# A fourth weight quarter taken for two token pairs at once: 512 columns in place of twice 256, and three zero products less

## Chip, core and metric

The kernel runs on one core of one Trainium2 chip. The time is that of one execution on the device in microseconds. TensorE (PE in the profile) makes all products, PEld is its loading of weights; VectorE is DVE, ScalarE is ACT, GpSimd is POOL, SyncE is SP.

## What is computed

Attention within chunks of 64 tokens, for 8 batches, 8 heads, 576 tokens and a head width of 64, and behind it a feed-forward part on the 4608 tokens of width 512:

```python
scores = scale * np.matmul(q_c, k_c.transpose(0, 1, 2, 4, 3))
attn = np.exp(scores - np.max(scores, axis=-1, keepdims=True))
attn = attn / (np.sum(attn, axis=-1, keepdims=True) + 1e-09)
x = np.matmul(attn, v_c)           # then (B, S, H * D) rows: 4608 x 512
a = x @ w1                         # 512 x 1024
b = x @ w2                         # 512 x 1024
out = (a * b @ w3) @ w_out         # 1024 x 1024, 1024 x 512
```

Inputs and output are float32; the products are made in bfloat16 with float32 sums.

## The kernel before

The tokens are cut into 18 pairs of 256 (p = 0 to 17; a pair is two units of 128, u = 0 and 1), and two pairs make a group of 512 tokens. The work is written out by hand as one list of steps, ORDER, which is walked from left to right; every engine and every DMA queue gets its instructions in that order. A step is a letter with numbers:

- `q`, `k`, `v`: loads of a pair, issued by POOL, with a cast to bfloat16. `i0` to `i3`: one quarter of the columns (256) of w1 and of w2 each. `h0`, `h1`: halves of w3, and `o`: w_out, each as four DMAs that fill 32 partitions each. POOL issues all of them in the order of the list.
- `R`, `K`: pair 0's q and k by another way (SP, ACT and a cast). `T`: VectorE transposes q (T p.0) or k (T p.1). `G`, `H`: moves on the SP queue, from pair 6 (MOVED) on.
- `S`: scores on TensorE; `E`: exponential on ScalarE; `P`: times v, on TensorE; `N`: VectorE divides; `X`: VectorE transposes to x with its width on the partitions, one unit at a time.
- `A p.j` and `B p.j`: x times w1 into the first PSUM bank of a tile, x times w2 into the second. `C`: ScalarE copies the first bank to SBUF; `M`: VectorE multiplies it with the second into the tile `ab` of the group (bfloat16).
- `V`, `W`, `Z`: w3 times w_out is made once (w3 transposed by VectorE in V, products on TensorE in W, copied in Z), so that `O` makes the output from `ab` with one product; `Y` copies it and `Q` stores it.
- `D which.p.j.n.cols`: n products of zeros on TensorE, into the PSUM tile that the next real step overwrites. Nothing reads them.

The width of w1 and w2 is 8 blocks of 128 (f = 0 to 7), their depth 4 blocks. For the pairs 0 to 3, a step A p.j or B p.j takes two blocks, f = 2j and 2j + 1 (the quarter j of the weights), for the 256 tokens of one pair: 8 products of 128x256, each with a weight load of its own. From pair 4 on, a step takes one block f = j for the 512 tokens of a group: 4 products of 128x512. Both fill one bank with 512 float32 per partition. PSUM is four tiles of two banks, taken in turn, so a step that begins such a tile waits for what read the tile four before it.

The helper `mm` (L97) makes every product, and `load` (L100) every load by POOL. The list around the change: the zero products D1.0.0.6.512 stand ahead of A0.0; A0.3, B0.3 (pair 0, fourth quarter) stand around S2, behind A0.2, A1.0, B0.2, A1.1, B1.0 and B1.1; A1.2, A1.3, B1.2 and B1.3 follow P2.

Of the kernel before, what the change touches and what calls it, by code (L numbers as in the profile page):

```python
# [7 lines left out]

ORDER = """
R0.0 R1.0 R0.1 R1.1 v0 D0.0.1.9.512 K0.0 K1.0 T0.0.0 K0.1 T0.1.0 K1.1 S0.0 T0.0.1 E0.0 T0.1.1 q1 k1  # L10
S0.1 i0 E0.1 P0.0 P0.1 T1.0 D0.1.0.6.512 v1 N0.0 T1.1 N0.1 X0.0 X0.1 i1 i2 S1 E1 D1.0.0.6.512 A0.0
C0.0 P1 B0.0 q2 N1.0 X1.0 N1.1 A0.1 C0.1 k2 B0.1 M0.0 A0.2 X1.1 A1.0 i3 C0.2 B0.2 M0.1 A1.1 v2 q3
B1.0 B1.1 M0.2 C1.0 C1.1 T2.0 k3 A0.3 C0.3 T2.1 S2 E2 B0.3 M1.0 M1.1 P2 M0.3 N2.0 N2.1 A1.2 C1.2
X2.0 A1.3 X2.1 C1.3 T3.0 B1.2 q4 T3.1 v3 k4 B1.3 A2.0 M1.2 C2.0 B2.0 S3 E3 T4.0 A2.1 M1.3 B2.1 M2.0
P3 A2.2 h0 N3.0 N3.1 B2.2 X3.0 A2.3 C2.1 C2.2 X3.1 o M2.1 C2.3 B2.3 A3.0 C3.0 M2.2 B3.0 V0 h1 A3.1
A3.2 q5 k5 C3.1 M2.3 B3.1 B3.2 v4 V1 C3.2 q6 T4.1 V2 V3 M3.0 W0 S4 k6 q7 M3.1 Z0 M3.2 V4 V5 W1 T5.0
Z1 W2 V6 V7 T5.1 W3 T6.0 E4 k7 q8 v5 Z2 A3.3 k8 q9 k9 Z3 S5 T6.1 T7.0 q10 T7.1 E5 v6 v7 C3.3 P4 B3.3
N4.0 X4.0 M3.3 O0 G3.0 N4.1 k10 Y0 G3.1 T8.0 O1 X4.1 P5 T8.1 Y1 O2 Q0 N5.0 N5.1 X5.0 v8 X5.1 A4.0 S6
E6 T9.0 T9.1 S7 B4.0 T10.0 Y2 q11 O3 C4.0 M4.0 Q1 E7 P6 v9 N6.0 A4.1 N6.1 C4.1 Y3 B4.1 A4.2 X6.0
M4.1 G4.0 A4.3 X6.1 C4.2 P7 N7.0 C4.3 B4.2 G4.1 k11 B4.3 N7.1 X7.0 A4.4 M4.2 B4.4 Q2 M4.3 C4.4 T10.1  # L20
M4.4 A4.5 C4.5 S8 B4.5 A4.6 C4.6 A4.7 E8 B4.6 Q3 C4.7 X7.1 B4.7 M4.5 q12 P8 H3.0 M4.6 S9 H3.1 M4.7
O4 E9 T11.0 Y4 P9 N8.0 O5 k12 N8.1 A6.0 B6.0 Y5 T11.1 G5.0 T12.0 A6.1 X8.0 N9.0 B6.1 C6.0 C6.1 T12.1
A6.2 q13 X8.1 B6.2 N9.1 X9.0 M6.0 k13 C6.2 v10 T13.0 v11 X9.1 M6.1 A6.3 M6.2 q14 G5.1 C6.3 A6.4 q15
B6.3 C6.4 B6.4 A6.5 S10 C6.5 B6.5 T13.1 M6.3 M6.4 A6.6 H4.0 E10 P10 H4.1 M6.5 S11 N10.0 B6.6 k14
N10.1 v12 A6.7 C6.6 E11 G6.0 P11 M6.6 N11.0 B6.7 X10.0 N11.1 A8.0 A8.1 B8.0 G6.1 C6.7 C8.0 B8.1 A8.2
B8.2 C8.1 M6.7 T14.0 q16 A8.3 M8.0 C8.2 M8.1 X10.1 M8.2 X11.0 Q4 q17 T14.1 H5.0 B8.3 C8.3 S12 S13
X11.1 A8.4 E12 C8.4 B8.4 k15 H5.1 M8.3 E13 v13 k16 A8.5 B8.5 P12 M8.4 k17 v14 T15.0 N12.0 N12.1 O6
A8.6 v15 C8.5 C8.6 T15.1 Y6 T16.0 B8.6 A8.7 M8.5 C8.7 P13 Q5 M8.6 B8.7 X12.0 A10.0 C10.0 B10.0 N13.0
N13.1 M8.7 G7.0 A10.1 T16.1 C10.1 A10.2 X12.1 X13.0 M10.0 C10.2 G7.1 B10.1 B10.2 A10.3 B10.3 C10.3
M10.1 T17.0 A10.4 C10.4 M10.2 M10.3 A10.5 T17.1 B10.4 M10.4 X13.1 v16 H6.0 S14 C10.5 S15 G8.0 B10.5  # L30
M10.5 O7 G8.1 E14 E15 P14 A10.6 H6.1 N14.0 C10.6 B10.6 A10.7 N14.1 Q6 Y7 M10.6 P15 N15.0 N15.1 C10.7
X14.0 S16 B10.7 M10.7 O8 E16 Q7 A12.0 B12.0 C12.0 M12.0 Y8 A12.1 C12.1 P16 S17 N16.0 X14.1 B12.1 E17
A12.2 M12.1 B12.2 A12.3 C12.2 A12.4 B12.3 X15.0 B12.4 v17 C12.3 M12.2 A12.5 N16.1 B12.5 M12.3 H7.0
X15.1 A12.6 X16.0 A12.7 C12.4 M12.4 C12.5 M12.5 C12.6 P17 N17.0 Q8 B12.6 B12.7 M12.6 H7.1 A14.0
A14.1 C12.7 B14.0 N17.1 C14.0 M12.7 O9 B14.1 C14.1 Y9 A14.2 X16.1 M14.0 M14.1 C14.2 A14.3 B14.2 Q9
O10 B14.3 X17.0 H8.0 Y10 Q10 A14.4 C14.3 A14.5 X17.1 C14.4 B14.4 M14.2 B14.5 H8.1 M14.3 A14.6 O11
Y11 B14.6 M14.4 O12 C14.5 C14.6 Y12 A14.7 M14.5 A16.0 C14.7 C16.0 Q11 M14.6 B14.7 A16.1 C16.1 A16.2
B16.0 B16.1 M14.7 M16.0 C16.2 M16.1 Q12 A16.3 O13 B16.2 B16.3 A16.4 C16.3 M16.2 Y13 M16.3 C16.4
A16.5 A16.6 B16.4 A16.7 C16.5 B16.5 M16.4 O14 Y14 C16.6 B16.6 C16.7 M16.5 B16.7 M16.6 Q13 M16.7 O15
Y15 O16 Q14 Q15 Y16 Q16 O17  # L40
"""


# [5 lines left out]
def first_path(  # L49
# [22 lines left out]
    FO = DF // P  # L72
# [19 lines left out]
    def inorder(ins):  # L92
        tc.keep_in_program_order(ins)
        return ins

    def mm(*a, **kw):
        return inorder(nc.tensor.matmul(*a, **kw))  # L97
# [4 lines left out]
    def psum(name):  # L102
        return ps.tile([P, 2, 512], f32, tag="p", name=name)
# [89 lines left out]
    qkT_t, qkm_t, s_t, e_t, pv_t, xn_t, xm_t, xt_t = {}, {}, {}, {}, {}, {}, {}, {}  # L193
# [101 lines left out]
    def new_xt(g):  # L295

        if g not in xt_t:
            xt_t[g] = asb.tile([P, KO * GT], bf, tag="xt", bufs=4, name="xt")
        return xt_t[g]
# [24 lines left out]
    ab_t, ps_t, a_t, o_t = {}, {}, {}, {}  # L324

    def do_D(which, p, j, n, cols):

        d, key = ((s_t, (p, (None, 0)[j])), (ps_t, (p, j)), (pv_t, (p, 0)))[which]
        if key not in d:
            d[key] = psum("z_ps")  # L330
        for _ in range(n):
            mm(d[key][:, 0, 0:cols], lhsT=zero[:, 0:P], rhs=zero[:, 0:cols], start=True, stop=True)

    def do_AB(p, j, f, which):

        if p >= MOVED:
            rhs = new_xt(p // 2)[:].rearrange("p (s o t) -> p o s t", s=2, o=KO)
        else:
            rhs = new_xt(p // 2)[:].rearrange("p (o t) -> p o t", o=KO)
            if p < 4:  # L340
                rhs = rhs[:, :, p % 2 * PT:(p % 2 + 1) * PT]
        fs = (f,) if p >= 4 else (2 * j, 2 * j + 1)
        n = GT // len(fs)
        for i, f in enumerate(fs):
            for ki in range(KO):
                ins = mm(ps_t[p, j][:, which, i * n:(i + 1) * n],
                         lhsT=(w1, w2)[which][:, ki, f * P:(f + 1) * P], rhs=rhs[:, ki],
                         start=(ki == 0), stop=(ki == KO - 1))
                if which == 1:
                    if (p, j) in first:  # L350
                        two_banks(ins, first[p, j])
                    else:
                        second.setdefault((p, j), []).append(ins)
# [3 lines left out]
    def two_banks(a, b):  # L357

        tc.declare_no_dep(a.ins, b.ins, reason="w1's product is read in one bank, w2's is made in the next")

    def do_A(p, j):
        ps_t[p, j] = ps_t.pop((p, j)) if (p, j) in ps_t else psum("ab_ps")
        do_AB(p, j, j, 0)

    def do_B(p, j):
        do_AB(p, j, j, 1)
# [7 lines left out]
    def do_M(p, j):  # L374
        g = p // 2
        if g not in ab_t:
            ab_t[g] = msb.tile([P, FO, GT], bf, tag="ab", bufs=3, name="ab")
        if p < 4:
            o = ab_t[g][:, 2 * j:2 * j + 2, p % 2 * PT:(p % 2 + 1) * PT]
            view = lambda t: t.rearrange("p (j t) -> p j t", j=2)  # L380
        elif p < MOVED:
            o = ab_t[g][:, j]
            view = lambda t: t
        else:
            o = ab_t[g][:, j].rearrange("p (c s y) -> p s c y", s=2, y=BL)
            view = lambda t: t.rearrange("p (s c y) -> p s c y", s=2, y=BL)
        inorder(nc.vector.tensor_mul(o, view(a_t.pop((p, j))[:]), view(ps_t.pop((p, j))[:, 1, :])))  # L387
# [66 lines left out]
    def load_half3(i):  # L454
# [9 lines left out]

    do = {"q": load_q, "k": load_k, "v": load_v, "i": load_w12, "o": load_wo, "h": load_half3, "T": do_T, "S": do_S, "R": do_R, "K": do_K, "E": do_E, "w": do_w, "x": do_x, "G": do_G, "H": do_H,
          "P": do_P, "N": do_N, "X": do_X, "A": do_A, "B": do_B, "C": do_C, "M": do_M, "D": do_D, "V": do_V,
          "W": do_W, "Z": do_Z, "O": do_O, "Y": do_Y, "Q": do_Q}
    for step in ORDER.split():
# [88 lines left out]
def kernel(tc, *args):  # L557
    second_path(tc, first_path(tc, *args), *args)
# [30 lines left out]
```

## Time and profile before

| | before |
|---|---|
| median of 3 runs | 241.46 us (240.96 to 241.86) |
| the profiled execution | 241.66 us, its span 240.1 us |
| mean granted TensorE clock | 0.985 |
| busy: PE, PEld, DVE | 230.6, 120.2, 152.3 us |
| busy: ACT, POOL | 84.7, 83.4 us |
| products ab_ps of 128x256, of 128x512 | 240, 448 |
| DMA moved | 39.21 MB |

The profile is one execution. A row of a timeline has the start, the length, the engine, the line, the operation with its output and inputs, their shape, the number of instructions in a row and, in brackets, the idle time ahead and what ended it. A name z_ps is a PSUM tile that zero products have opened. A product's end is modelled, so the length of a group holds a tail behind the last one. "A <- B: t, n, m" in the waits reads: A waited for B, t us in total, n times, m the longest. In the table of stretches stand, behind the stretch, its length, the busy time and count of PE, PEld, DVE, ACT and POOL, the granted clock, the DMA share and GB/s. "DMA to landing" is the time from the issue of a load to its last byte.

### The profile page before, as it was taken

The page shows a single profiled execution, that of the slowest core. Times are in us where ns is not written, and L with a number is a line of the kernel's source. Part 1 is how long each engine was busy: PE and PEld are TensorE (multiplying, and loading weights), DVE is VectorE, ACT ScalarE, POOL GpSimd, SP SyncE. Part 2 cuts the span into 40 slices and gives each one's busy share as a digit, 9 for nine tenths or more (in the row PEclk, how much of TensorE's full clock was granted, in tenths as well). Part 3 has the DMA queues.
Part 4 walks back from the last instruction along what each step waited for, and adds up shares of the span by engine and source line. Part 5 has one row for each costly group of instructions (what it writes and reads, how often), then busy time and mean ns, then how long its engine had stood idle before and what let it go on. Part 6 is the DMA issues. An engine that isn't in the chain of part 4 may idle for free.

```text
span 240.1 us, 6225 instructions
## 1 busy us (share of the span) xinstructions
PE 230.6 (96%) x2621; PEld 120.2 (50%) x2621; DVE 152.3 (63%) x237; ACT 84.7 (35%) x119; POOL 83.4 (35%) x112
## 2 busy tenths in 40 slices
PE   5699999999999999999999999999999999999994
PEld 1367788744645444444544444454444444444442
DVE  2766799959979596998599798474773222223200
ACT  4322334214412544333526143355332213521322
POOL 7846865647852424775543520000000000000000
PEclk9679999999999999999999999999999999999999
DMA  6999999999999999999999999860410442202224
GB/s 177 179 185 188 178 175 199 202 188 174 174 220 242 236 224 253 201 204 196 212 222 222 214 252 152 190 210 3 131 48 3 131 131 87 90 0 89 85 90 175
DMA packets 94397, 39.21 MB, mean 163 GB/s; under 512 B 75296, under 2 KB 86816, under 8 KB 94368
## 3 DMA queue, kind: packets, MB, share of 16 engines
q0 software_dynamic: 82592, 18.88, 84.8%
q1 hardware_dynamic: 10720, 19.41, 27.6%
q10 hardware_dynamic: 1056, 0.52, 0.8%
q8 instruction: 20, 0.33, 0.5%
q14 instruction: 9, 0.07, 0.1%
HBM read 38.80 MB, written 9.44 MB: 201 GB/s over the span
## 4 chain that ended last, share of the span: by engine, by line
PE 55%; DMA 31%; POOL 5%; DVE 3%; issue 2%; SPq 2%; ACT 1%; DVEq 0%; POOLq 0%
PE ab_ps L97 34%; PE o_ps L97 17%; DMA qk<-in_k_dram 17%; DMA w<-in_moe_w_dram 7%; DMA qk<-in_q_dram 4%; DMA qkm<-qkT 3%; POOL vbuf L100 2%; SPq L199 2%; PE s_ps L97 2%; POOL qk L100 2%; PE pv L97 2%; DVE ab L387 1%; POOL w L100 1%; DVE xn L272 1%; DVE qkT L207 1%
## 5 line engine op out<-in xcount | busy, mean ns | idle before, releaser
L97 PE MATMUL ab_ps<-xt,w 128*128 128x512 bf16 (+1 forms) x688 | 128.7, 342 | 0.5 <-DMA w<-in_moe_w_dram 0.5
L97 PEld LDWEIGHTS <-w 128*128 128x128 bf16 x704 | 67.0, 98 | 54.9 <-DMA w<-in_moe_w_dram 1.3
L387 DVE TENSOR_TENSOR ab<-a_sb,ab_ps 128x512 bf16<-128x512 f32 x71 | 47.0, 673 | 53.8 <-PE ab_ps L97 30.2
L370 ACT COPY a_sb<-ab_ps 128x512 f32<-128x512 f32 x71 | 41.4, 587 | 73.8 <-PE ab_ps L97 73.0
L97 PE MATMUL o_ps<-w3o,ab 128*128 128x512 bf16 (+2 forms) x296 | 64.8, 373 | 0.5 <-issue 0.3
L207 DVE STREAM_TRANSPOSE qkT<-qk 128x1024 bf16<-128x1024 bf16 (+1 forms) x38 | 45.8, 1232 | 5.5 <-ACT qk L150 3.7
L97 PEld LDWEIGHTS <-ab 128*128 128x128 bf16 x296 | 28.4, 98 | 33.6 <-issue 1.0
L100 POOL DMA_DIRECT2D vbuf<-in_v_dram x40 | 33.8, 847 | 23.2 <-DMA qk<-in_k_dram 5.9
L417 ACT COPY o_sb<-o_ps 128x1024 f32<-128x1024 f32 x17 | 17.2, 1014 | 43.8 <-PE o_ps L97 43.4
L272 DVE TENSOR_TENSOR xn<-pv,rcs 128x512 bf16<-128x512 f32 x36 | 24.9, 691 | 1.2
L100 POOL DMA_DIRECT2D qk<-in_q_dram x23 | 18.0, 783 | 15.8 <-DVE ab L387 4.8
L100 POOL DMA_DIRECT2D qk<-in_k_dram x23 | 17.9, 781 | 11.1 <-DMA qk<-in_k_dram 4.1
L240 ACT ACTIVATE e<-s_ps 128x1024 bf16<-128x1024 f32 (+1 forms) x17 | 16.9, 1000 | 11.4 <-PE s_ps L97 11.2
L313 DVE STREAM_TRANSPOSE xm<-xn 128x512 bf16<-128x512 bf16 x24 | 16.3, 689 | 0.1
L97 PE MATMUL w_ps<-wo,w3T 128*128 128x512 bf16 x64 | 14.1, 379 | 0.1
L269 DVE RECIPROCAL rcs<-pv 128x8 f32<-128x8 f32 x36 | 6.9, 192 | 11.4 <-PE pv L97 11.4
L291 POOL CROSS_LANE_REDUCE all_good<-good 128x1 f32<-128x1 f32 x1 | 0.4, 354 | 39.6 <-DVE both L289 39.6
L100 POOL DMA_DIRECT2D w<-in_moe_w_dram x16 | 11.1, 696 | 5.7 <-DMA w<-in_moe_w_dram 3.9
L97 PEld LDWEIGHTS <-e 64*32 64x32 bf16 (+1 forms) x768 | 7.8, 101 | 6.9 <-issue 4.4
L428 DVE STREAM_TRANSPOSE w3T<-w 128x1024 bf16<-128x1024 bf16 x8 | 9.5, 1210 | 2.4 <-DMA w<-in_moe_w_dram 2.4
L97 PE MATMUL pv<-vbuf,e 64*32 64x65 bf16 (+1 forms) x768 | 10.1, 198 | 0.3 <-ACT e L240 0.2
L97 PEld LDWEIGHTS <-w3T 128*128 128x128 bf16 x64 | 6.1, 98 | 7.5 <-issue 0.4
(28 smaller groups left out, 56.3 us busy)
## 6 DMA issues: line engine op xcount, KB each, us to landing
out_dram<-o_sb SPq DMA_DIRECT2D x17, 512.0 KB, 3.0
qkm<-qkT SPq DMA_DIRECT2D x48, 128.0 KB, 7.0
vbuf<-in_v_dram POOLq DMA_DIRECT2D x32, 128.0 KB, 11.1
w<-in_moe_w_dram POOLq DMA_DIRECT2D x16, 256.0 KB, 9.1
xt<-xm SPq DMA_DIRECT2D x48, 64.0 KB, 5.8
qk<-in_q_dram POOLq DMA_DIRECT2D x11, 256.0 KB, 9.0
qk<-in_k_dram POOLq DMA_DIRECT2D x11, 256.0 KB, 12.1
wo<-in_moe_w_out_dram POOLq DMA_DIRECT2D x4, 256.0 KB, 9.4
```

What stands on the lines that cost most here:

```text
L97: return inorder(nc.tensor.matmul(*a, **kw))
L100: return inorder(nc.gpsimd.dma_start(dst, src))
L199: inorder(nc.sync.dma_start(dst, src))
L207: inorder(nc.vector.transpose(qkT_t[g][:, :, p % 2, s, heads(h)].rearrange("p e h (y t) -> p h t e y", t=2), qk_t[p][:, s, heads(h)].rearr ...
L240: inorder(nc.scalar.activation(e_t[p][:, :, heads(hh)], s_t[p, hh][:].rearrange("p u (h q) -> p u h q", q=CH)[:, :, heads(hh)], Exp, scale ...
L269: inorder(nc.vector.reciprocal(rc, pv[:, :, :, D:W]))
L272: inorder(nc.vector.tensor_mul(xn_t[p][:, u], pv[:, :, :, 0:D], rc.to_broadcast([P, 2, 4, D])))
L313: inorder(nc.vector.transpose(xm_t[g][:, u, :, m].rearrange("p o (c y) -> p c o y", y=BL), xn_t[p][:].rearrange("p u r m d -> p (u r) m d" ...
L370: first[p, j] = inorder(nc.scalar.copy(a_t[p, j][:], ps_t[p, j][:, 0, :]))
L387: inorder(nc.vector.tensor_mul(o, view(a_t.pop((p, j))[:]), view(ps_t.pop((p, j))[:, 1, :])))
L417: inorder(nc.scalar.copy(o_sb[:], ps_t.pop(p)[:]))
L428: inorder(nc.vector.transpose(w3T_t[f][:].rearrange("p k (f y) -> p f k y", y=BL), w3[:, NB * f:NB * (f + 1), :].rearrange("p f (k x) -> p ...
```

## The change

For the pairs 0 to 3 a step A, B, C or M with j of 4 or more now stands for the whole group: it takes one block, f = j - 4, in 512 columns. So A0.10 and A0.11 are the blocks 6 and 7 (the fourth quarter) for the pairs 0 and 1 together. In the list, A1.2 with its B, C and M stands where A0.3 stood, A0.10 where A1.2 stood, and A0.11 where A1.3 stood; A0.3 and A1.3 are gone. The pairs 2 and 3 keep their steps. D1.0.0 makes three zero products instead of six. The new form of the key in `do_D` gives the same keys for the steps in the list.

```diff
-S0.1 i0 E0.1 P0.0 P0.1 T1.0 D0.1.0.6.512 v1 N0.0 T1.1 N0.1 X0.0 X0.1 i1 i2 S1 E1 D1.0.0.6.512 A0.0
+S0.1 i0 E0.1 P0.0 P0.1 T1.0 D0.1.0.6.512 v1 N0.0 T1.1 N0.1 X0.0 X0.1 i1 i2 S1 E1 D1.0.0.3.512 A0.0
 C0.0 P1 B0.0 q2 N1.0 X1.0 N1.1 A0.1 C0.1 k2 B0.1 M0.0 A0.2 X1.1 A1.0 i3 C0.2 B0.2 M0.1 A1.1 v2 q3
-B1.0 B1.1 M0.2 C1.0 C1.1 T2.0 k3 A0.3 C0.3 T2.1 S2 E2 B0.3 M1.0 M1.1 P2 M0.3 N2.0 N2.1 A1.2 C1.2
-X2.0 A1.3 X2.1 C1.3 T3.0 B1.2 q4 T3.1 v3 k4 B1.3 A2.0 M1.2 C2.0 B2.0 S3 E3 T4.0 A2.1 M1.3 B2.1 M2.0
-P3 A2.2 h0 N3.0 N3.1 B2.2 X3.0 A2.3 C2.1 C2.2 X3.1 o M2.1 C2.3 B2.3 A3.0 C3.0 M2.2 B3.0 V0 h1 A3.1
+B1.0 B1.1 M0.2 C1.0 C1.1 T2.0 k3 A1.2 C1.2 T2.1 S2 E2 B1.2 M1.0 M1.1 P2 M1.2 N2.0 N2.1 A0.10 C0.10
+X2.0 A0.11 X2.1 C0.11 T3.0 B0.10 q4 T3.1 v3 k4 B0.11 A2.0 M0.10 C2.0 B2.0 S3 E3 T4.0 A2.1 M0.11 B2.1
+M2.0 P3 A2.2 h0 N3.0 N3.1 B2.2 X3.0 A2.3 C2.1 C2.2 X3.1 o M2.1 C2.3 B2.3 A3.0 C3.0 M2.2 B3.0 V0 h1
...
     def do_D(which, p, j, n, cols):
-        d, key = ((s_t, (p, (None, 0)[j])), (ps_t, (p, j)), (pv_t, (p, 0)))[which]
+        d, key = ((s_t, (p, 0 if j == 1 else None)), (ps_t, (p, j)), (pv_t, (p, 0)))[which]
...
+    def single(p, j):
+        return p < 4 and j < FO // 2
+
     def do_AB(p, j, f, which):
+        if j >= FO // 2 and p < 4:
+            f = j - FO // 2
...
-            if p < 4:
+            if single(p, j):
                 rhs = rhs[:, :, p % 2 * PT:(p % 2 + 1) * PT]
-        fs = (f,) if p >= 4 else (2 * j, 2 * j + 1)
+        fs = (2 * j, 2 * j + 1) if single(p, j) else (f,)
...
     def do_M(p, j):
-        if p < 4:
+        if single(p, j):
             o = ab_t[g][:, 2 * j:2 * j + 2, p % 2 * PT:(p % 2 + 1) * PT]
             view = lambda t: t.rearrange("p (j t) -> p j t", j=2)
         elif p < MOVED:
-            o = ab_t[g][:, j]
+            o = ab_t[g][:, j - FO // 2 if p < 4 else j]
```

More of the change, by code (lines that the diff above doesn't have):

```diff
@@ L15 @@
-P3 A2.2 h0 N3.0 N3.1 B2.2 X3.0 A2.3 C2.1 C2.2 X3.1 o M2.1 C2.3 B2.3 A3.0 C3.0 M2.2 B3.0 V0 h1 A3.1
[L16 to L40, printed above, removed]
+B1.0 B1.1 M0.2 C1.0 C1.1 T2.0 k3 A1.2 C1.2 T2.1 S2 E2 B1.2 M1.0 M1.1 P2 M1.2 N2.0 N2.1 A0.10 C0.10
@@ new lines @@
+X2.0 A0.11 X2.1 C0.11 T3.0 B0.10 q4 T3.1 v3 k4 B0.11 A2.0 M0.10 C2.0 B2.0 S3 E3 T4.0 A2.1 M0.11 B2.1
+M2.0 P3 A2.2 h0 N3.0 N3.1 B2.2 X3.0 A2.3 C2.1 C2.2 X3.1 o M2.1 C2.3 B2.3 A3.0 C3.0 M2.2 B3.0 V0 h1
+A3.1 A3.2 q5 k5 C3.1 M2.3 B3.1 B3.2 v4 V1 C3.2 q6 T4.1 V2 V3 M3.0 W0 S4 k6 q7 M3.1 Z0 M3.2 V4 V5 W1
+T5.0 Z1 W2 V6 V7 T5.1 W3 T6.0 E4 k7 q8 v5 Z2 A3.3 k8 q9 k9 Z3 S5 T6.1 T7.0 q10 T7.1 E5 v6 v7 C3.3 P4
+B3.3 N4.0 X4.0 M3.3 O0 G3.0 N4.1 k10 Y0 G3.1 T8.0 O1 X4.1 P5 T8.1 Y1 O2 Q0 N5.0 N5.1 X5.0 v8 X5.1
@@ new lines @@
+A4.0 S6 E6 T9.0 T9.1 S7 B4.0 T10.0 Y2 q11 O3 C4.0 M4.0 Q1 E7 P6 v9 N6.0 A4.1 N6.1 C4.1 Y3 B4.1 A4.2
+X6.0 M4.1 G4.0 A4.3 X6.1 C4.2 P7 N7.0 C4.3 B4.2 G4.1 k11 B4.3 N7.1 X7.0 A4.4 M4.2 B4.4 Q2 M4.3 C4.4
+T10.1 M4.4 A4.5 C4.5 S8 B4.5 A4.6 C4.6 A4.7 E8 B4.6 Q3 C4.7 X7.1 B4.7 M4.5 q12 P8 H3.0 M4.6 S9 H3.1
+M4.7 O4 E9 T11.0 Y4 P9 N8.0 O5 k12 N8.1 A6.0 B6.0 Y5 T11.1 G5.0 T12.0 A6.1 X8.0 N9.0 B6.1 C6.0 C6.1
+T12.1 A6.2 q13 X8.1 B6.2 N9.1 X9.0 M6.0 k13 C6.2 v10 T13.0 v11 X9.1 M6.1 A6.3 M6.2 q14 G5.1 C6.3
@@ new lines @@
+A6.4 q15 B6.3 C6.4 B6.4 A6.5 S10 C6.5 B6.5 T13.1 M6.3 M6.4 A6.6 H4.0 E10 P10 H4.1 M6.5 S11 N10.0
+B6.6 k14 N10.1 v12 A6.7 C6.6 E11 G6.0 P11 M6.6 N11.0 B6.7 X10.0 N11.1 A8.0 A8.1 B8.0 G6.1 C6.7 C8.0
+B8.1 A8.2 B8.2 C8.1 M6.7 T14.0 q16 A8.3 M8.0 C8.2 M8.1 X10.1 M8.2 X11.0 Q4 q17 T14.1 H5.0 B8.3 C8.3
+S12 S13 X11.1 A8.4 E12 C8.4 B8.4 k15 H5.1 M8.3 E13 v13 k16 A8.5 B8.5 P12 M8.4 k17 v14 T15.0 N12.0
+N12.1 O6 A8.6 v15 C8.5 C8.6 T15.1 Y6 T16.0 B8.6 A8.7 M8.5 C8.7 P13 Q5 M8.6 B8.7 X12.0 A10.0 C10.0
+B10.0 N13.0 N13.1 M8.7 G7.0 A10.1 T16.1 C10.1 A10.2 X12.1 X13.0 M10.0 C10.2 G7.1 B10.1 B10.2 A10.3
@@ new lines @@
+B10.3 C10.3 M10.1 T17.0 A10.4 C10.4 M10.2 M10.3 A10.5 T17.1 B10.4 M10.4 X13.1 v16 H6.0 S14 C10.5 S15
+G8.0 B10.5 M10.5 O7 G8.1 E14 E15 P14 A10.6 H6.1 N14.0 C10.6 B10.6 A10.7 N14.1 Q6 Y7 M10.6 P15 N15.0
+N15.1 C10.7 X14.0 S16 B10.7 M10.7 O8 E16 Q7 A12.0 B12.0 C12.0 M12.0 Y8 A12.1 C12.1 P16 S17 N16.0
+X14.1 B12.1 E17 A12.2 M12.1 B12.2 A12.3 C12.2 A12.4 B12.3 X15.0 B12.4 v17 C12.3 M12.2 A12.5 N16.1
+B12.5 M12.3 H7.0 X15.1 A12.6 X16.0 A12.7 C12.4 M12.4 C12.5 M12.5 C12.6 P17 N17.0 Q8 B12.6 B12.7
+M12.6 H7.1 A14.0 A14.1 C12.7 B14.0 N17.1 C14.0 M12.7 O9 B14.1 C14.1 Y9 A14.2 X16.1 M14.0 M14.1 C14.2
@@ L41 @@
+A14.3 B14.2 Q9 O10 B14.3 X17.0 H8.0 Y10 Q10 A14.4 C14.3 A14.5 X17.1 C14.4 B14.4 M14.2 B14.5 H8.1
+M14.3 A14.6 O11 Y11 B14.6 M14.4 O12 C14.5 C14.6 Y12 A14.7 M14.5 A16.0 C14.7 C16.0 Q11 M14.6 B14.7
+A16.1 C16.1 A16.2 B16.0 B16.1 M14.7 M16.0 C16.2 M16.1 Q12 A16.3 O13 B16.2 B16.3 A16.4 C16.3 M16.2
+Y13 M16.3 C16.4 A16.5 A16.6 B16.4 A16.7 C16.5 B16.5 M16.4 O14 Y14 C16.6 B16.6 C16.7 M16.5 B16.7
+M16.6 Q13 M16.7 O15 Y15 O16 Q14 Q15 Y16 Q16 O17
 """
```

## The prediction, made before the changed kernel had run

> **What bounds the kernel now.** I read the page's busy line and slices first, then TensorE's waits, TensorE's order of time around the change, and last the loads that its waits name.
>
> ```profile
> span 240.1 us, 6225 instructions
> PE 230.6 (96%) x2621; PEld 120.2 (50%) x2621; DVE 152.3 (63%) x237; ACT 84.7 (35%) x119; POOL 83.4 (35%) x112
> PE   5699999999999999999999999999999999999994
> PEclk9679999999999999999999999999999999999999
> ```
>
> TensorE is busy for 96% of the span, and the slices (6 us each) show its idle time at the two ends. The granted clock (PEclk, in tenths) is low in the second and third slice alone. So the kernel is bound by TensorE's work, plus whatever short waits stand in its row. The change lies at 14 us and between 26 and 36 us; which waits of TensorE stand near there and behind?
>
> ```profile
> PE ab_ps L97 <- DMA w<-in_moe_w_dram: 0.5, 2, 0.3
> PE s_ps L97 <- DMA qkm<-qkT: 0.4, 1, 0.4
> ```
>
> One line is for the weights w1 and w2 (two waits), one for the moved q and k of a later group. TensorE in order of time (start, length, what; idle before and its releaser in brackets):
>
> ```profile
> 14.02 1.70 PE L97 MATMUL z_ps<-zero 128*128 128x512 bf16 x6
> 15.56 1.04 PE L97 MATMUL z_ps<-xt,w 128*128 128x256 bf16 x8
> 18.04 2.10 PE L97 MATMUL ab_ps<-xt,w 128*128 128x256 bf16 x16
> 20.43 5.42 PE L97 MATMUL ab_ps<-xt,w 128*128 128x256 bf16 x48 [0.29 <-DMA w<-in_moe_w_dram]
> 26.04 1.05 PE L97 MATMUL ab_ps<-xt,w 128*128 128x256 bf16 x8 [0.20 <-DMA w<-in_moe_w_dram]
> 27.02 0.71 PE L97 MATMUL s_ps<-qkT 32*64 32x64 bf16 x64
> 28.87 0.70 PE L97 MATMUL pv<-vbuf,e 64*32 64x65 bf16 x64 [0.16 <-ACT e L240]
> 29.50 5.41 PE L97 MATMUL ab_ps<-xt,w 128*128 128x256 bf16 x48
> 38.22 8.91 PE L97 MATMUL ab_ps<-xt,w 128*128 128x256 bf16 x80
> 47.25 3.61 PE L97 MATMUL w_ps<-wo,w3T 128*128 128x512 bf16 x16
> 139.07 10.54 PE L97 MATMUL ab_ps<-xt,w 128*128 128x512 bf16 x48
> ```
>
> The length of a group holds the tail of its last product, so I take the pace from differences: (8.91 - 5.41) / 32 = 0.109 us (0.1094) for 256 columns, and (10.54 - 3.61) / 32 = 0.217 us (0.2166) for 512. The group at 18.04 is A0.1 and B0.1; the one at 20.43 is A0.2, A1.0, B0.2, A1.1, B1.0, B1.1; the one at 26.04 is A0.3; 27.02 is S2, 28.87 is P2, and 47.25 is W0, the first product of w3 and w_out. A0.2 and A0.3 each begin when a quarter of w1 lands; nothing on TensorE sets their time.
>
> **Three zero products fewer.** They stand ahead of A0.0. Which clock do they run at, and what is A0.0's next condition?
>
> ```profile
> 7.60:7.80 0.20, 0.00 (x0) 0.00 (x0) 0.20 (x2) 0.20 (x1) 0.20 (x1) 0.77 1.99 174
> 13.00:14.00 1.00, 1.00 (x65) 0.93 (x64) 0.97 (x3) 0.00 (x0) 0.36 (x1) 0.50 2.19 153
> 14.20:14.60 0.40, 0.40 (x2) 0.15 (x1) 0.40 (x2) 0.40 (x1) 0.00 (x0) 0.58 2.44 155
> 14.60:14.80 0.20, 0.20 (x3) 0.10 (x1) 0.20 (x1) 0.20 (x1) 0.00 (x0) 1.00 2.25 164
> 13.68 1.29 DVE L305 STREAM_TRANSPOSE xt<-xn 128x512 bf16<-128x512 bf16 x2
> ```
>
> The third number from the end of a stretch is the granted clock: it falls near 7.7, is 0.50 until about 14.53 (0.58 over 14.20 to 14.60 is 0.33 us at 0.50 and 0.07 at 1.00), then 1.00. At half speed a product takes 2 x 0.217 = 0.43 us, so of the six the first ends at 14.45, the second, partly at full clock, at about 14.71, and four at 0.217 follow to 15.56, as the trace has it. With three, the last ends at 14.92. A0.0 then waits for X0.1, whose transposes end at 13.68 + 1.29 = 14.97; with some 0.07 us for the signal it starts near 15.05, 0.51 us earlier. Of 0.65 us of products, 0.14 becomes idle.
>
> Next come P1 (after E1), B0.0, A0.1, B0.1 and A0.2. Their weights land when they did:
>
> ```profile
> 19.08 0.77 PEld L97 LDWEIGHTS <-w 128*128 128x128 bf16 x8 [0.29 <-DMA w<-in_moe_w_dram]
> 20.42 5.14 PEld L97 LDWEIGHTS <-w 128*128 128x128 bf16 x48 [0.57 <-DMA w<-in_moe_w_dram]
> 17.98 0.76 POOL L100 DMA_DIRECT2D w<-in_moe_w_dram  x1 [0.57 <-DMA w<-in_moe_w_dram]
> ```
>
> B0.1's weights arrive at 19.08 and A0.2's at 20.42, both awaited already: A0.1 was through at 18.04 + 8 x 0.1094 = 18.92, 0.16 before, and B0.1 at 19.96, 0.47 before A0.2 began. The loads are issued by POOL, which waits for earlier loads to land (the last row, the fourth quarter's first issue), not for TensorE. So the 0.51 us is all waited away at A0.2: this part is worth 0 at 20.43. If A0.2 were not held, it would be worth up to 0.51.
>
> By the Trainium skill ("TensorE: Matmul & The Clock Gate", Part 1: The HAM clock gate) the clock is released after about 3.4 us of sustained activity, counted in a free-running window, which speaks against removing work that keeps TensorE warm. Here the three removed products lie after the rise at 14.53, so by the trace they did not earn it; what the rule would make of another phase is the clock rival below.
>
> **The fourth quarter in 512 columns.** A0.3, B0.3, A1.3 and B1.3 (32 products of 256 columns, 32 weight loads) become A0.10, B0.10, A0.11 and B0.11 (16 of 512, 16 loads): 32 x 0.1094 = 3.50 against 16 x 0.2166 = 3.47 us, a gain of 0.03, because the loads already ran beside the products. C and M stay four, each over 512 columns as before; PSUM tiles, DMAs and the other engines' steps keep number and order. M0.10 writes one row of 512 instead of two of 256, which I price at nothing; either form is bounded by M's 0.65 to 0.69 us.
>
> **The new order.** A1.2 stands where A0.3 stood. It needs the third quarter, which B0.2 used at about 22, and X1. So the wait for the fourth quarter at 26.04 goes: the 48 products from 20.43 are through at 20.43 + 48 x 0.1094 = 25.68, and A1.2 starts then, 0.36 us earlier. Then S2 could start at 26.56 instead of 26.92, if its transposes are through:
>
> ```profile
> 23.93 2.48 DVE L207 STREAM_TRANSPOSE qkT<-qk 128x1024 bf16<-128x1024 bf16 x2
> ```
>
> They end at 26.41, so 0.15 us is left. E2, B1.2 and P2 follow S2 as before, P2's short wait for E2 with them; A0.10 comes after P2, at about 29.1, three microseconds after its weights (26.0). So from 26 to 47 us TensorE is 0.36 + 0.03 = 0.39 us early; the ends are 0, if S2 or the next transposes hold it back, and 0.39, which I take, as no row holds it.
>
> **What is late next.** W0 needs all four quarters of w_out, since each fills 32 of the 128 partitions, and V0 needs the whole first half of w3. Their last loads:
>
> ```profile
> 35.87 1.71 POOL L100 DMA_DIRECT2D wo<-in_moe_w_out_dram  x3 [0.37 <-DMA vbuf<-in_v_dram]
> L100 POOL DMA_DIRECT2D wo<-in_moe_w_out_dram x1: 576/576/576, 37.0 to 37.0; - x1
> DMA to landing us min/median/max: 10.1/10.1/10.1
> ...
> L100 POOL DMA_DIRECT2D w<-in_moe_w_dram x1: 642/642/642, 33.7 to 33.7; - x1
> DMA to landing us min/median/max: 8.3/8.3/8.3
> ```
>
> The first three rows are w_out's, the last two w3's. w_out is complete at 37.0 + 10.1 = 47.1, and W0 starts at 47.25, though the 80 products ahead of it were through at 38.22 + 80 x 0.1094 = 46.97. So W0 stood waiting for 0.28 us for a load that POOL issued when an earlier load landed. If TensorE arrives 0.39 earlier, it waits 0.67 and W0 starts at 47.25 again. The whole gain of this change on TensorE ends there; nothing on TensorE goes round this wait.
>
> What can still pass is what runs beside it. V0's data land at 33.7 + 8.3 = 42.0, and from V0 the chain of waits leads on:
>
> ```profile
> 42.18 1.21 DVE w3T L428
> ...
> 44.38 0.87 POOL qk L100
> 45.25 10.11 DMA qk<-in_k_dram
> ...
> 106.38 7.69 DMA qkm<-qkT
> ...
> 114.20 0.67 PE s_ps L97 x31
> ```
>
> VectorE could reach V0 0.39 earlier, but the load lets it begin only about 0.1 earlier; the loads of pair 5 follow 0.1 earlier, and TensorE's wait of 0.4 us for qkm, which ends at 114.20, where this chain meets it, could shrink by that 0.1. The ends are 0 and 0.4; I take 0.1, since the load's landing leaves no more.
>
> **The sum.** Zero products 0 (up to -0.51), order and width 0 at W0 (up to -0.39), the later wait -0.1: 241.66 - 0.1 = 241.56 us for the profiled execution (span 240.1, 1.56 us around it). That execution stood 0.2 above the median of the runs, 241.46; on the median the forecast is 241.36, told as **241.4 us**. 0.5% is 1.2 us, about what a measurement of this kernel can tell from no change (its three runs lie within 240.96 to 241.86).
>
> **Rivals.**
>
> *The gains come through.* If in the runs that are timed the loads land earlier than in this trace, the waits at 20.43 and 47.25 hold nothing, and 0.51 + 0.39 = 0.90 us come through, with the 0.1 at most 1.0: 240.5 us (241.46 - 1.0), or 241.1 if only the second wait gives way. For it: W0's wait is only 0.28 us long. Against it: both waits are in the trace, each on a load whose issue waits for other loads. As 240.5 is 0.4% below before, only a little more, in the transfers, makes it faster by over 0.5%.
>
> *Transfers collide later (slower).* If POOL's loads from 44.38 on go out earlier, the move of q and k at 106.38 shares its way with more of them. It took 7.69 us; POOL's loads took between 8.3 us (w3's fourth above) and 10.1 us (w_out's last) here, by how much was under way. A move that takes 10.1 - 8.3 = 1.8 us longer reaches TensorE at 115.9 instead of 114.06, and nothing later makes that good, as TensorE is busy from there on: 241.46 + 1.8 = 243.3 us. It decides as soon as the move lands later than 114.06, since S waits for it already. Against it: the order of all issues is the same, and the shift is only 0.1 us.
>
> *The clock rises later (slower).* If the three products were needed, the clock would stay at 0.50 for some time after 14.53. From 14.92 on, half of that time is lost. The waits for loads give 0.51 + 0.16 + 0.47 = 1.14 us of it back by A0.2, and those at A1.2's place and at W0 another 0.36 + 0.28. Another 3.4 us (half of the 6.8 from fall to rise), to 17.9, loses 1.5 us and costs nothing; 6.8 us, to 21.3, loses 3.2 and costs 3.2 - 1.14 - 0.64 = 1.4 us: 242.9 us. It decides from a rise after 14.92 + 2 x 1.78 = 18.5 us. Against it: with three products TensorE's row has no gap beyond the 0.14 us ahead of A0.0. By the same section of the Trainium skill the clock falls again only after an idle window; the trace agrees, in that PEclk stays at 9 or more over all the short waits from the fourth slice on.
>
> *The change doesn't do what it says.* X0.1 is late in the changed kernel, and the three products turn into idle time ahead of A0.0: 241.5 us, as before.
>
> **How the numbers follow.** Forecast 0.53, all within 0.5%. Gains come through 0.27: 0.17 faster by over 0.5%, 0.10 within. Transfers collide 0.10, slower. Clock 0.05: 0.03 slower, 0.02 within. Not what it says 0.05, within. Together: faster 0.17, same 0.53 + 0.10 + 0.02 + 0.05 = 0.70, slower 0.13. The range reaches down to the 240.5 of the first rival and, for the scatter of the runs, 0.1 further, 240.4; upward to 242.2, the highest run shown (241.86) and part of the way to the slower rivals. Below it lies some 0.08, above it 0.12.
>
> **What would show it.** In the changed profile: A0.0 near 15.05; A0.2 again near 20.4, with a longer wait for w ahead of it; no wait for w near 26; P2 near 28.5 and 256-column and 512-column products in the old total of time; W0 again near 47.2, after about 0.67 us of waiting; S near 114.1. I am wrong if W0 starts earlier than 47.0 and what follows keeps that lead to the end, or if TensorE gets a wait of over 1 us between 50 and 165 us that is not there now.

## The result, and the profile after

| | before | after |
|---|---|---|
| median of 22 runs each | 241.75 us | 241.09 us |
| ratio, 95% interval | | 0.9973 (0.9961 to 0.9986) |
| profiled execution, span | 241.66, 240.1 us | 240.88, 239.3 us |

The changed kernel is faster by 0.27%, 0.66 us between the medians. The forecast was a gain of 0.1 us, within 0.5%; the direction and that bound held, and the gain is some six times the one worked out. All ratios here are taken over the runs within 1.5% of the fastest of their kernel, which leaves out five of all runs below, four of them of the kernel before with six instructions more. The page after, and TensorE's waits:

```profile
span 239.3 us, 6187 instructions
PE 229.9 (96%) x2602; PEld 118.2 (49%) x2602; DVE 152.5 (64%) x237; ACT 84.6 (35%) x119; POOL 83.6 (35%) x112
```

```profile
PE w_ps L97 <- DMA wo<-in_moe_w_out_dram: 0.8, 1, 0.8
PE ab_ps L97 <- DMA w<-in_moe_w_dram: 0.6, 2, 0.3
PE pv L97 <- DMA vbuf<-in_v_dram: 0.4, 1, 0.4
```

The first wait is W0's for w_out, which before had no row of its own; the wait for moved q and k (s_ps) is gone. TensorE in order of time in the changed kernel (start, length, idle before in brackets):

```profile
10.27 2.74 PE L97 MATMUL z_ps<-zero 128*128 128x512 bf16 x6
13.94 0.82 PE L97 MATMUL z_ps<-zero 128*128 128x512 bf16 x3
15.01 1.03 PE L97 MATMUL z_ps<-xt,w 128*128 128x256 bf16 x8 [0.24 <-DVE xt L305]
18.85 1.05 PE L97 MATMUL ab_ps<-xt,w 128*128 128x256 bf16 x8 [0.28 <-DMA w<-in_moe_w_dram]
20.19 6.30 PE L97 MATMUL ab_ps<-xt,w 128*128 128x256 bf16 x56 [0.30 <-DMA w<-in_moe_w_dram]
28.28 0.41 PE L97 MATMUL pv<-vbuf,e 64*32 64x65 bf16 x32 [0.16 <-ACT e L240]
29.06 0.32 PE L97 MATMUL pv<-vbuf,e 64*32 64x65 bf16 x32 [0.37 <-DMA vbuf<-in_v_dram]
37.73 8.91 PE L97 MATMUL ab_ps<-xt,w 128*128 128x256 bf16 x80
47.45 3.61 PE L97 MATMUL w_ps<-wo,w3T 128*128 128x512 bf16 x16 [0.82 <-DMA wo<-in_moe_w_out_dram]
114.09 0.45 PE L97 MATMUL s_ps<-qkm 64*64 64x64 bf16 x32
131.76 3.63 PE L97 MATMUL o_ps<-w3o,ab 128*128 128x512 bf16 x16
```

A0.0 starts at 15.01 after a short wait for X0.1, A0.2 at 20.19 after a wait for its weights, and the fourth quarter is awaited no more: 56 products follow without a gap. At 37.73 + 80 x 0.1094 = 46.48 the products ahead of W0 are through, 0.49 earlier than before, and W0 starts at 47.45, 0.20 later than before. So at 47 us nothing is gained. In these two executions the gain lies behind it, at two places of the profile of before:

```profile
113.62 0.21 PE L97 MATMUL s_ps<-qkm 64*64 64x64 bf16 x1
114.20 0.67 PE L97 MATMUL s_ps<-qkm 64*64 64x64 bf16 x31 [0.37 <-DMA qkm<-qkT]
...
132.09 1.69 PE L97 MATMUL o_ps<-w3o,ab 128*128 128x512 bf16 x7
134.07 2.10 PE L97 MATMUL o_ps<-w3o,ab 128*128 128x512 bf16 x9 [0.30 <-issue]
```

In S near 114 us the first of 32 products ran, and the others waited for moved q and k until 114.87; without the wait it is 0.45 us in all, as after, so 0.80 us were lost. In O5, 16 products took from 132.09 to 136.17, 4.08 us against 3.63 after: 0.45 lost, with no releaser that the profile shows ("issue"). With W0's +0.20 and a wait of 0.27 in an S at 77 us, which of the two only the profile after has, the sum is 0.20 + 0.27 - 0.80 - 0.45 = -0.78, the whole difference of the two executions. One pair of traces doesn't tell which of these belongs to the kernels and which to the execution.

### The profile page after: what moved, and what is told of

It reads as the page before. It is cut to its first block, busy times and chain, and to the rows that moved or that the text cites. A ratio compares the mean times of both kernels' runs of the same rounds, so it can differ in the third digit from the quotient of the medians.

```text
span 239.3 us, 6187 instructions
## 1 busy us (share of the span) xinstructions
PE 229.9 (96%) x2602; PEld 118.2 (49%) x2602; DVE 152.5 (64%) x237; ACT 84.6 (35%) x119; POOL 83.6 (35%) x112
## 4 chain that ended last, share of the span: by engine, by line
PE 78%; DMA 15%; POOL 4%; issue 1%; DVE 0%; ACT 0%; DVEq 0%; POOLq 0%
PE ab_ps L97 42%; PE o_ps L97 26%; DMA w<-in_moe_w_dram 7%; PE w_ps L97 6%; DMA wo<-in_moe_w_out_dram 4%; DMA vbuf<-in_v_dram 3%; PE s_ps L97 2%; PE pv L97 2%; POOL vbuf L100 2%; POOL w L100 1%; POOL qk L100 1%; POOL wo L100 0%; DVE ab L393 0%; ACT o_sb L416 0%; DVE o_sb L416 0%
## 5 line engine op out<-in xcount | busy, mean ns | idle before, releaser
L97 PEld LDWEIGHTS <-w 128*128 128x128 bf16 x688 | 65.3, 98 | 56.9 <-DMA w<-in_moe_w_dram 1.1
```

## Experiments

My theory, "gate": what TensorE gains before W0 is waited away where loads land. Its first rivals were that the parts add up, or that W0's wait costs nothing in the end. For what comes behind W0 there were two more, after the first traces had shown the same stall twice: "place", that the stall in O5 comes with the number of TensorE instructions ahead of it, and "chance", that the late stalls and waits differ from execution to execution.

**Each part alone.** First the zero products, then the order with the 512 columns:

```diff
 (kernel before)  -D1.0.0.6.512  +D1.0.0.3.512
 (kernel after)   -D1.0.0.3.512  +D1.0.0.6.512
```

> The kernel before with three zero products fewer ahead of A0.0 and nothing else. Theory 'gate' (all that TensorE gains before W0 is waited away where loads land): A0.0 0.5 us earlier, A0.2 again when its quarter of w1 lands (20.2 to 20.4), W0 again near 47.3; time 0.0 us to -0.1 us against before. Rival 'parts add up' (each part passes to the end by its share of the measured -0.66 us): -0.2 to -0.5 us.

> The changed order and the 512 columns, with six zero products as before. Theory 'gate': no wait for w near 26, S2 some 0.4 us earlier, W0 again near 47.3 after 0.6 to 0.8 us of waiting; time 0.0 to -0.2 us against before. Rival 'parts add up': -0.2 to -0.5 us, so that this and the zero products alone make up -0.66 together.

Measured: zero products alone 0.9976 (0.9947 to 1.0005), order and width alone 0.9965 (0.9944 to 0.9986). The rows of the first, then of the second:

```profile
20.08 5.66 PE L97 MATMUL ab_ps<-xt,w 128*128 128x256 bf16 x48 [0.30 <-DMA w<-in_moe_w_dram]
47.39 3.61 PE L97 MATMUL w_ps<-wo,w3T 128*128 128x512 bf16 x16 [0.43 <-DVE w3T L428]
```

```profile
20.10 6.30 PE L97 MATMUL ab_ps<-xt,w 128*128 128x256 bf16 x56 [0.28 <-DMA w<-in_moe_w_dram]
47.40 3.61 PE L97 MATMUL w_ps<-wo,w3T 128*128 128x512 bf16 x16 [0.64 <-DMA wo<-in_moe_w_out_dram]
```

A0.2 and W0 stand about where they stood, as "gate" has it. (For W0's wait in the first the profile names VectorE; w_out's last load, issued at 36.9, lands there 10.3 us later, near 47.2.) But each part alone measured about the whole gain, 0.24% and 0.35% or some 0.6 and 0.85 us, where "gate" had promised at most 0.1 and 0.2 us, though neither moves W0 forward. The intervals are as wide as the gains, and the first holds 1: the times by themselves don't exclude that the parts add up. What speaks against it is where W0 stands.

**The gate taken away.** Pair 4's k is loaded behind w_out, so that w_out lands earlier; in the changed kernel, and in the kernel before:

```diff
-... q4 T3.1 v3 k4 ... X3.1 o M2.1 ...
+... q4 T3.1 v3 ... X3.1 o k4 M2.1 ...
```

> The changed kernel with pair 4's k loaded behind w_out instead of ahead of w3's first half (256 KB fewer ahead of w_out, at some 190 GB/s 1.3 us). Theory 'gate': w_out lands near 46.0 instead of 47.3, W0 starts when TensorE comes to it, near 46.6 instead of 47.45; time 0.5 to 0.9 us below the changed kernel, if no later load holds it. Rival 'W0's wait costs nothing in the end' (a later load, such as w3's second half or the move of q and k near 114 us, sets the time): W0 earlier, and the time as that of the changed kernel within 0.2 us.

> The kernel before with pair 4's k loaded behind w_out. Theory 'gate': TensorE comes to W0 at 47.0 and starts it there, 0.3 us earlier than before; time -0.2 to -0.3 us against before, and 0.4 to 0.6 us above the changed kernel with the same load order, since there the gain of the change passes W0. Rival 'W0's wait costs nothing in the end': time as before within 0.2 us.

Measured: 0.9978 (0.9955 to 1.0002) and 1.0002 (0.9973 to 1.0031). Changed kernel, then kernel before:

```profile
46.45 3.62 PE L97 MATMUL w_ps<-wo,w3T 128*128 128x512 bf16 x16
51.74 0.70 PE L97 MATMUL s_ps<-qkT 32*64 32x64 bf16 x64 [1.67 <-DVE ab L393]
```

```profile
46.78 3.62 PE L97 MATMUL w_ps<-wo,w3T 128*128 128x512 bf16 x16
51.64 0.70 PE L97 MATMUL s_ps<-qkT 32*64 32x64 bf16 x64 [1.24 <-DVE ab L387]
```

W0 now starts when TensorE comes to it, and the changed kernel comes 0.33 us earlier: the lead that the change makes before 47 us is real, and w_out's landing had held it. The times that "gate" promised against its base, -0.5 to -0.9 and -0.2 to -0.3 us, did not come. The lead ends at S4 (51.74 against 51.64), which waits for VectorE behind the late k. A second step frees that too, by putting the transpose of that k behind M3.0 on VectorE:

```diff
 (changed kernel, k4 behind o)
-... C3.2 q6 T4.1 V2 V3 M3.0 W0 S4 ...
+... C3.2 q6 V2 V3 M3.0 T4.1 W0 S4 ...
```

> The changed kernel with pair 4's k loaded behind w_out, and T4.1 (its transpose) behind M3.0 on VectorE, so that S4's tile is free before that load is awaited. Theory 'gate': W0 near 46.5, S4 near 50.1 instead of 51.0, and TensorE 0.5 to 0.9 us ahead of the changed kernel at S4; if w3's second half (landing near 53) does not hold W2, the lead lasts, time 240.2 to 240.6. Rival 'the next load takes it': W2 waits for V4, near 54.5, and the lead is under 0.3 us from there on.

Measured: 0.9974 (0.9950 to 0.9997), the ratio of the changed kernel.

```profile
46.62 3.62 PE L97 MATMUL w_ps<-wo,w3T 128*128 128x512 bf16 x16
50.80 3.63 PE L97 MATMUL w_ps<-wo,w3T 128*128 128x512 bf16 x16
54.88 7.08 PE L97 MATMUL w_ps<-wo,w3T 128*128 128x512 bf16 x32 [0.45 <-DVE w3T L434]
```

W1 at 50.80 is 0.84 ahead of the changed kernel (51.64), W2 at 54.88 only 0.22 ahead (51.64 + 16 x 0.2166 = 55.11): the next load, w3's second half, takes the lead, as the rival had said. No version in these runs beats the changed kernel clearly.

**What lies behind W0.** The kernel before once more, the kernel before with six TensorE instructions more at its start, and the changed kernel with 38 more, which puts its later instructions back at their old numbers:

```diff
 (before, again: no edit)
 (before)   -D0.0.1.9.512  +D0.0.1.12.384
 (changed)  -D0.0.1.9.512  +D0.0.1.28.164
```

> The kernel before, run once more beside itself. Theory 'place' (a short stall of TensorE at one place of its instruction stream, 0.2 to 0.5 us ahead of the ninth weight load of O5, comes with the number of its instructions): the stall stands there again, near 134 us. Rival 'chance' (the later stalls of the first profile differ from execution to execution): it is gone or elsewhere. Time: ratio 1.000 within 0.2%.

> The kernel before with the first nine zero products of 512 columns made as twelve of 384: the same 4608 columns, and six TensorE instructions more (three weight loads, three products) ahead of everything else; nothing reads them. Theory 'place': the stall ahead of the ninth weight load of O5 near 134 us is gone or moves by six instructions, time -0.2 to -0.5 us against before. Theory 'gate' with chance behind W0: time as before within 0.1 us, W0 near 47.3.

> The changed kernel with the first nine zero products of 512 columns made as 28 of 164 (4592 columns in place of 4608): 38 TensorE instructions more, so that its later instructions stand at the numbers that they had before the change. Theory 'place': the stall ahead of the ninth weight load of O5 is back, time 0.2 to 0.5 us above the changed kernel, near before. Theory 'gate' with chance behind W0: no such stall, time as the changed kernel.

Measured: 1.0013 (0.9989 to 1.0037), 1.0020 (0.9996 to 1.0045), 0.9994 (0.9970 to 1.0019). The kernel before, again:

```profile
47.44 3.61 PE L97 MATMUL w_ps<-wo,w3T 128*128 128x512 bf16 x16 [0.56 <-DMA wo<-in_moe_w_out_dram]
114.12 0.45 PE L97 MATMUL s_ps<-qkm 64*64 64x64 bf16 x32
131.79 1.69 PE L97 MATMUL o_ps<-w3o,ab 128*128 128x512 bf16 x7
133.77 2.10 PE L97 MATMUL o_ps<-w3o,ab 128*128 128x512 bf16 x9 [0.30 <-issue]
```

The changed kernel with its old numbers:

```profile
132.77 1.69 PE L97 MATMUL o_ps<-w3o,ab 128*128 128x512 bf16 x7
134.90 2.10 PE L97 MATMUL o_ps<-w3o,ab 128*128 128x512 bf16 x9 [0.44 <-issue]
```

The stall in O5 stands again at the same product, nine of sixteen left, and it is back in the changed kernel when 38 instructions are added at its start. Its ratio is then 0.9994 and no longer 0.9973, but the intervals overlap, and the trace has more than this stall in it:

```profile
14.88 0.22 PE L97 MATMUL z_ps<-qkT 32*64 32x64 bf16 x3 [0.87 <-issue]
114.71 0.67 PE L97 MATMUL s_ps<-qkm 64*64 64x64 bf16 x31 [0.48 <-DMA qkm<-qkT]
```

Its span is 1.6 us longer than the changed kernel's (240.9 against 239.3): 0.60 in O5, and some 0.9 in S near 114 us, which ends at 115.38 instead of 114.54 though it begins 0.07 earlier. A second stall without a releaser, 0.87 us in S1, is gone again at W0 (47.54). The kernel before with k4 late, which has the old count too, shows it ahead of the same weight load:

```profile
132.24 3.89 PE L97 MATMUL o_ps<-w3o,ab 128*128 128x512 bf16 x16
...
134.03 1.61 PEld L97 LDWEIGHTS <-ab 128*128 128x128 bf16 x8 [0.38 <-issue]
```

The wait for moved q and k at 114 us is not there in the second execution of the same kernel: that one is of the execution. The kernel before with six instructions more had no stall in O5, but a new long wait for moved q and k, and was not faster; "place" had promised 0.2 to 0.5 us, and missed:

```profile
129.46 0.93 PE L97 MATMUL s_ps<-qkm 64*64 64x64 bf16 x63 [1.47 <-DMA qkm<-qkT]
```

**Four more on the same question.** Two instructions fewer in the kernel before; its six more once again; six more in the changed kernel; the changed kernel again.

```diff
 (before)   -D1.0.0.6.512  +D1.0.0.5.512
 (before)   -D0.0.1.9.512  +D0.0.1.12.384
 (changed)  -D0.0.1.9.512  +D0.0.1.12.384
 (changed, again: no edit)
```

> The kernel before with one zero product fewer ahead of A0.0 (five in place of six): two TensorE instructions fewer, and 0.2 us of products, which the load that A0.2 waits for takes up. Theory 'place': the stall ahead of the ninth weight load of O5 is gone, time -0.3 to -0.5 us against before. Theory 'chance': time as before within 0.2 us, the waits for moved q and k differing from run to run.

> The kernel before with twelve zero products of 384 in place of nine of 512 at the start, once more. Theory 'place': no stall in O5 again, and the 1.5 us wait for moved q and k near 128 us that the first profile showed is not there again, time below before by 0.2 to 0.5 us. Rival (the longer stream itself costs time, whatever the place): time again 0.2 to 0.5 us above before.

> The changed kernel with the same twelve zero products of 384 at the start: 6 instructions more than it has, 32 fewer than before the change. Theory 'place': no stall in O5, time as the changed kernel within 0.2 us. Rival (instructions at the start cost time by themselves): 0.3 us or more above the changed kernel.

> The changed kernel once more. Theory 'place' and 'gate' together: W0 near 47.4 after 0.5 to 0.8 us of waiting for w_out, no stall in O5, time 0.4 to 0.8 us below before. Theory 'chance': the waits for moved q and k come at other places, and the time is within 0.3 us of before.

Measured, in this order: 0.9994 (0.9970 to 1.0018), 1.0032 (0.9994 to 1.0070), 0.9961 (0.9943 to 0.9980), 0.9976 (0.9955 to 0.9997). O5 has no stall in any of the four; S near 114 us waits in the first two. Their rows, first to third:

```profile
114.03 0.87 PE L97 MATMUL s_ps<-qkm 64*64 64x64 bf16 x32
132.12 3.63 PE L97 MATMUL o_ps<-w3o,ab 128*128 128x512 bf16 x16
```

```profile
114.34 0.67 PE L97 MATMUL s_ps<-qkm 64*64 64x64 bf16 x31 [0.57 <-DMA qkm<-qkT]
132.23 3.63 PE L97 MATMUL o_ps<-w3o,ab 128*128 128x512 bf16 x16
```

```profile
47.51 3.61 PE L97 MATMUL w_ps<-wo,w3T 128*128 128x512 bf16 x16 [0.87 <-DMA wo<-in_moe_w_out_dram]
131.85 3.63 PE L97 MATMUL o_ps<-w3o,ab 128*128 128x512 bf16 x16
```

The changed kernel again:

```profile
47.44 3.61 PE L97 MATMUL w_ps<-wo,w3T 128*128 128x512 bf16 x16 [0.87 <-DMA wo<-in_moe_w_out_dram]
131.62 3.63 PE L97 MATMUL o_ps<-w3o,ab 128*128 128x512 bf16 x16
```

Over all 14 traces: the stall stands in each of the four with the TensorE count of the kernel before, and in none of the ten with another. It costs 0.26 (k4 late), 0.45, 0.45 and 0.60 us. The time mostly follows it: seven results without the stall (the changed kernel twice, each part alone, the changed kernel with k4 late, with both gates and with six instructions more) lie at 0.9961 to 0.9978, three with it at 0.9994 to 1.0013. But the kernel before with two instructions fewer gave 0.9994, whose interval holds both 1 and the gain expected, and the one with six more gave 1.0020 and 1.0032, its runs spread from 240.6 to 245.9 us. The longer start by itself doesn't cost that, since the changed kernel with the same six lost nothing (0.9961). Something else goes with the time just as well: a wait of some 0.4 us or more for moved q and k, near 114 or 128 us, stands in five of the seven traces of kernels that were not faster, and in none of the seven that were; each of the slower seven has the wait, the stall or both. No run takes that wait away by itself. So the place of the stall is shown; that it alone makes the 0.66 us is not, and what brings the wait is open.

The cleanest pair is the kernel before again against the changed kernel. They stand within 0.03 us of each other at W0 (47.44, 47.45), at S near 114 (114.12, 114.09) and at O5's start (131.79, 131.76), and the spans end 0.6 us apart (239.9, 239.3): 0.45 of that is the stall in O5, and the rest comes in small steps behind it.

## Why the prediction was right, and where it was not

- **Zero products: right.** A0.0 was forecast for 15.05 and came at 15.01, with the idle time for X0.1 ahead; A0.2 still waits for its weights, in the changed kernel and with this edit alone.
- **Order and width: right in the mechanism, one wait missed.** The wait at 26 us went, and S2 moved from 27.02 to 26.43. P2, forecast near 28.5, began at 28.28, but its second half waited 0.37 us for pair 2's v to land (the row at 29.06), which the prediction did not count. A0.10 so began some 0.2 us late against the forecast 29.1.
- **W0 swallows the lead: right.** Forecast 47.25 after 0.67 us of waiting, measured 47.45 after 46.48, 0.97; the page counts 0.82 because a product's length holds its tail. In the nine other runs whose loads stand in the old order, among them both parts alone, W0 starts between 47.20 and 47.72. When w_out comes earlier, the lead of 0.33 us appears.
- **The size: luck in part.** The forecast holds because its range was wide; no term of its sum explains a gain of 0.66 us. One rival, "the gains come through", has 241.1 us in it, which is the time measured, but W0 at 47.45 shows that it is not what happened.
- **The later wait, -0.1: the step that failed.** It was to pass from V0 through pair 5's loads to the wait near 114 us. It didn't: in the changed kernel V0 and those loads are later than before (42.18 and 44.38 there):

```profile
42.21 1.25 DVE L434 STREAM_TRANSPOSE w3T<-w 128x1024 bf16<-128x1024 bf16 x1 [0.46 <-DMA w<-in_moe_w_dram]
...
44.59 0.89 POOL L100 DMA_DIRECT2D qk<-in_q_dram  x1 [1.48 <-DVE ab L393]
```

And the wait near 114 us itself is missing in the second execution of before. What the sum left out, and the traces show, is the stall of 0.45 us in O5: it stood in the profile of before as 0.30 us of "issue", and the edits reach it by changing the number of instructions ahead of it. Whether it carries the rest of the 0.66 us is not shown.

- **The rivals.** Gains that come through ahead of W0: none in any trace. Transfers that collide later: such waits of 0.4 to 1.5 us near 114 and 128 us do appear, in five of the 14 traces, but in neither of the changed kernel itself. The clock: not later in the changed kernel, where the three zero products took 0.82 us from 13.94 on, the full pace. That the clock falls only after an idle window is borne out by the late waits, but not near 7.7 us: there it fell within a wait of 1.3 us for VectorE; a wait of 1.7 us stood before it, and products from 6.61 on between the two.

## What to carry to other kernels

A gain on the busiest engine lasts only if it passes the next place where a load lands; look for the last load of each tile that all partitions need, and add its time to landing to its issue. When both halves of a change seem to give the same gain alone, look for what they share before crediting the work of either, here the number of instructions ahead of a place; and when one cause seems found, look whether another goes with the same runs. A second trace of the same kernel is worth more than another reading of the first, since it tells which waits belong to the execution.

## What the runs showed of the hardware

- A stall of 0.26 to 0.60 us without a releaser stands at one product of TensorE's stream and goes when the instructions ahead are 2, 6 or more fewer or 6 more. By the Trainium skill ("Runtime: NRT & Kernel Launch", Instruction fetch mechanics) instructions come in blocks of 256, and crossing into a block is mostly hidden. That would fit a stall tied to a number, and would be a crossing that isn't hidden. The traces speak for it. The profile lists transfers of instructions too, 20 of 16 KB in before (queue and kind, then packets, MB, and their share of 16 engines' time):

```profile
q8 instruction: 20, 0.33, 0.5%
```

In the four traces with the stall one of them starts at 131.61, 131.32, 131.66 (k4 late) and 132.56, and the instruction behind the stall follows 2.46, 2.45, 2.36 and 2.33 us later. The second stall of the changed kernel with 38 more ends 2.44 us behind such a start, at 12.43. In the ten other traces TensorE comes to the same number of its stream, its 3738th weight load or product, 2.43 to 8.34 us behind such a start, and does not stop. So TensorE stalls in O5 where, without the stall, it would have come 1.7 to 2.1 us behind the transfer's start, and not where it comes later. No run moves the transfer by itself: that it is the cause is argued, not shown.
- The time at which the zero products begin to run at full pace differs from execution to execution of one kernel: the six from about 10.3 us took 2.74 us in the first profile of before, all at half pace, and in the second:

```profile
10.33 2.11 PE L97 MATMUL z_ps<-zero 128*128 128x512 bf16 x6
```

(2.74 - 2.11) / 0.217 is 2.9 products' worth of half pace less, so the pace rose near 11.7 instead of 14.5 us. By the Trainium skill ("TensorE: Matmul & The Clock Gate", Part 1: The HAM clock gate) the window is free-running; the traces agree, as far as the time of the rise differs between executions. It costs nothing here, since the loads set A0.2's time either way.
- The granted clock of a stretch (third number from the end) does not always fit the pace: in the changed kernel it reads 1.00 while the six zero products at 10.27 took 2.74 us, the half pace:

```profile
10.30:13.00 2.70, 2.70 (x11) 0.69 (x7) 2.67 (x5) 0.00 (x0) 1.31 (x3) 1.00 1.49 200
```
